# Rebuilt weights made twice as fast, in bursts, and a block's sums taken in three loops, in a linear attention with two feed-forward networks

## The chip, the cores and the metric

The kernel runs on one core of one Trainium2 chip. The metric is the device time of one execution in microseconds (us), as the median of several runs. The engines are named as the profile names them: PE is TensorE (matmul), PEld its weight load, DVE is VectorE, ACT is ScalarE, POOL is GpSimd, and SP is SyncE, whose queue starts nearly all transfers here. Matmuls write to PSUM, which the kernel uses as eight banks of 128 x 512 fp32.

## The reference

A random-feature attention over 4 batches, 8 heads, 576 positions and 64 columns is followed by two feed-forward networks (FFNs) over its 2304 rows of 512.

```
proj = einsum('bhsd,md->bhsm', x, omega);  h = proj - sum(x*x)/2
phi(x) = exp(h - max(h)) / sqrt(128)                  # x = q or k, scaled
kv = einsum('bhsm,bhsd->bhmd', phi(k), v);  z = sum(phi(k), axis=2)
attn = einsum('bhsm,bhmd->bhsd', phi(q), kv) / (phi(q) . z + 1e-6)
x = attn as 2304 x 512
FFN 1: h = x @ w_in (512 x 2048);  g = relu(h)**2;  y = g @ w_out (2048 x 512)
FFN 2: the same with its own weights and g = h if h > 0 else exp(h) - 1
```

The weights of the FFNs come as 64-bit floats, all else as 32-bit floats.

## The kernel before

**Precision.** Each fp32 operand of a large matmul is split into a high and a low limb (`xh`/`xl`, `gh`/`gl`, `wh`/`wl`), and a product is made of three matmuls: high by high, high by low, low by high. The high limb is a copy on ACT, the low limb a subtraction on DVE in the helper `minus` (line 74 in the profile).

**Weights.** The weights are cut into 64 parts (FFN, slice f of 16, and 0 for `w_in` or 1 for `w_out`), each 128 x 512 in 512 KB. `fetch` transfers a part into one of three buffers `st`. A part is then made up in three phases. Phase 0, `make_rebiased`, is one ACT instruction (L122, `cm`). Phase 1, `make_floats`, is three DVE instructions (L129, L130, L133, `cv`), after which the transfer of a later part is issued. Phase 2, `make_limbs`, is the copy to `wh` on ACT (L144) and the subtraction to `wl` on DVE (L74).

**Steps.** The FFNs' work is a list of steps (FFN, group g of 4, block of rows i with its first column n0, slice j of 4). A name such as `gf1_1_0_0_2` carries these five numbers: FFN 1 (the second one), group 1, block 0, column 0, slice 2. In the text a step is written in the same order, and the two networks are "FFN 1" and "FFN 2". A group holds eight parts, and its blocks are four of 512 columns and one of 256 (block 4, which comes second). In the very first group three blocks are taken in halves. `gemm1` of a step makes twelve matmuls into one PSUM bank (`ph`), then an epilogue: r, gf and gh/gl in FFN 1; gf, r, t on ACT, then r and gf on DVE, gh on ACT and gl on DVE in FFN 2. `gemm2` of a step, two steps later, adds twelve matmuls to four PSUM banks (`py`), and after the block's fourth slice the four banks are copied or summed on DVE into pages `ya`. After the last group of FFN 1 the sums become the limbs `xh`/`xl` of FFN 2's input. `moe_pieces` yields after each gemm, so a half step is twelve matmuls.

**Order.** Every engine runs its instructions in the order in which this program text issues them; no scheduler moves them. During attention a list of stages runs once a tick, and from some tick on each tick takes half steps as well. A half step may be followed by phases of weight work: `make(n, phases)` runs a phase if its turn is possible for a part below n. Parts that no gemm uses any more are counted in `n_dead`, and the main loop makes parts up to `n_dead` + 12. `need` makes a missing part on the spot. When a group of eight parts ends, eight new parts may be made.

**Banks.** The eight PSUM banks are handed out in turn to whatever asks next. In the FFNs the four `py` of a block whose `gemm2` starts take, in turn, the banks of three earlier `ph` (free when the epilogue has read them, in FFN 2 with DVE's gf) and of the first `py` of the block before (free when DVE has copied or summed it); the next `ph` takes the second.

Of the kernel before, what the change touches and what calls it, by code (L numbers as in the profile page):

```python
# [12 lines left out]
ALU = mybir.AluOpType  # L13
# [4 lines left out]
def linear_attention_two_ffn_kernel(  # L18
# [12 lines left out]
    nc = tc.nc  # L31
    P = 128
    B, H, S, D = q.shape
# [9 lines left out]
    GF = 4  # L43
    NG = NF // GF
    BLKS = [C * P] * B + [B * L]
# [18 lines left out]
    def page(shape, name, dt=F32):  # L64
        return pages.tile([P] + list(shape), dt, tag="page", name=name)

    def psum(name):
        return ps.tile([P, W], F32, tag="bank", name=name)

    def flat(t):  # L70
        return t.rearrange("p a b -> p (a b)")

    def minus(eng, out, whole, hi):
        eng.tensor_tensor(out=out, in0=whole, in1=hi.bitcast(F32), op=ALU.subtract)  # L74
# [5 lines left out]
    xh, xl = {}, {}  # L80

    def x_pages(moe, i, c, name):

        per = W // BLKS[i]
        for d, s in ((xh, "h"), (xl, "l")):
            if (moe, i, c // per) not in d:
                d[moe, i, c // per] = page([per, BLKS[i]], f"x{s}{moe}_{i}_{c // per}", F32R)
# [7 lines left out]
    parts = [(moe, f, o) for moe in range(2) for f in range(NF) for o in range(2)]  # L95
    parts[:2 * GF] = sorted(parts[:2 * GF], key=lambda p: (p[1] + LOOK * p[2], p[2]))
    staged, w_t = {}, {}
    n_fetched, n_made, n_dead = [0], [0, 0, 0], [0]

    def fetch(n):  # L100
        while n_fetched[0] < min(n, len(parts)):
            moe, f, o = p = parts[n_fetched[0]]
            w = WS[moe][o].bitcast(U32)
            t = stg.tile([P, W, 2], U32, tag="st", name=f"st{moe}_{f}_{o}")
            if o == 0:
                nc.sync.dma_start(
                    out=t.rearrange("p (c f) t -> p c (f t)", c=KD),
                    in_=w[:, f * 2 * P:(f + 1) * 2 * P].rearrange("(c p) f -> p c f", p=P),
                )
            else:  # L110
                nc.sync.dma_start(out=t.rearrange("p f t -> p (f t)"), in_=w[f * P:(f + 1) * P, :])
            staged[p] = t
            n_fetched[0] += 1
# [31 lines left out]
        minus(nc.vector, l, tf, h)  # L145
        w_t[p] = h, l

    def make(n, phases=(2, 1, 0)):

        n = min(n, len(parts))  # L150
        for c in phases:
            if n_made[c] < (n if c == 0 else n_made[c - 1]):
                (make_rebiased, make_floats, make_limbs)[c](n_made[c])
                n_made[c] += 1

    def need(p):
        while p not in w_t:
            make(parts.index(p) + 1)
        return w_t[p]


# [7 lines left out]
    def omega_limbs():  # L169
        nc.vector.tensor_copy(out=om[:, 1, :], in_=om[:, 0, :])  # L170
        p_om = psum("p_om")
        nc.tensor.transpose(p_om[:, :P], flat(om), ident)
        omT = page([2, M], "omT")
        nc.vector.memset(omT, 0.0)
        for j in range(2):
            nc.vector.tensor_scalar(
                out=omT[j * D:(j + 1) * D, j, :], in0=p_om[j * D:(j + 1) * D, :M], scalar1=SCALE, scalar2=None, op0=ALU.mult
            )
        nc.vector.tensor_copy(out=omh, in_=flat(omT))
        minus(nc.vector, oml, flat(omT), omh)  # L180
# [10 lines left out]
    def load(u):  # L191
        b, kind, hp = u
        t = page([8, D], f"ld{b}{kind}{hp}")
        st[u] = {"x": t}
        if kind == "l":
            for n, src in enumerate((k, q)):
                for i in range(LH):
                    nc.sync.dma_start(out=t[i * L:(i + 1) * L, n * NP:(n + 1) * NP, :], in_=left(src, b, i))
        else:
            nc.sync.dma_start(  # L200
                out=t.rearrange("p (h c) d -> p h (c d)", h=2),
                in_=(k if kind == "k" else q)[b, 2 * hp:2 * hp + 2, :C * P, :].rearrange(
                    "h (p c) d -> p h (c d)", c=C
                ),
            )
# [188 lines left out]
    def order(moe, g):  # L394
        whole = [(i, 0, BLKS[i]) for i in range(NB)]
        if (moe, g) == (0, 0):
            return [(i, n, n + W // 2) for i in range(B - 1) for n in (0, W // 2)] + whole[B - 1:]
        if (moe, g) == (1, NG - 1):
            return whole
        return whole[:1] + whole[B:] + whole[1:B]  # L400

    steps = [(moe, g, o, j) for moe in range(2) for g in range(NG) for o in order(moe, g) for j in range(GF)]
    g_t, y_t, ya_t = {}, {}, {}

    def gemm1(moe, g, o, j):
        i, n0, n1 = o
        n = n1 - n0
        nm = f"{moe}_{g}_{i}_{n0}_{j}"
        f = g * GF + j
        ih, il = need((moe, f, 0))  # L410
        ph = psum(f"ph{nm}")
        m = 0
# [29 lines left out]
    def gemm2(moe, g, o, j):  # L442
        i, n0, n1 = o
        n = n1 - n0
        f = g * GF + j
        oh, ol = need((moe, f, 1))
        gh, gl = g_t.pop((moe, g, o, j))
        nt = KD if moe == 0 else n // P
        cols = n if moe == 0 else DM
        per = W // cols  # L450
        if j == 0:
            for t in range(nt // per):
                y_t[t] = psum(f"py{moe}_{g}_{i}_{n0}_{t}")
        for t in range(nt):
            ts = slice(t * P, (t + 1) * P)
            y = y_t[t // per][:, t % per * cols:(t % per + 1) * cols]
            for m, (a, w) in enumerate(((gh, oh), (gh, ol), (gl, oh))):
                nc.tensor.matmul(  # L458
                    y, *((w[:, ts], a) if moe == 0 else (a[:, ts], w)),
                    start=j == 0 and m == 0 and t % per == 0, stop=j == GF - 1 and m == 2, skip_group_check=per > 1,  # L460
                )
        if o == order(moe, g)[-1]:
            n_dead[0] += 1
        if j < GF - 1:
            return
        last = g == NG - 1
        for t in range(nt // per):
            yv = y_t[t]
            if moe == 0 and n < BLKS[i]:
                assert g == 0  # L470
                for u in range(per):
                    c = t * per + u
                    if n0 == 0:
                        ya_t[i, c] = page([W], f"ya{moe}_{i}_{c}")
                    nc.vector.tensor_copy(out=ya_t[i, c][:, n0:n1], in_=yv[:, u * n:(u + 1) * n])
                continue
            if g == 0:
                ya = ya_t[i, t] = page([W], f"ya{moe}_{i}_{t}")
                nc.vector.tensor_copy(out=ya, in_=yv)
                continue  # L480
            ya = ya_t[i, t]
            nc.vector.tensor_tensor(out=ya, in0=yv, in1=ya, op=ALU.add)  # L482
            if not last:
                continue
            ya_t.pop((i, t))
            if moe == 0:
                x_pages(1, i, t * per, "y")
                hi, lo = flat(xh[1, i, t]), flat(xl[1, i, t])
                nc.scalar.copy(out=hi, in_=ya)
                minus(nc.vector, lo, ya, hi)  # L490
            elif i < B:
                nc.sync.dma_start(
                    out=out[i * S:i * S + C * P, :].rearrange("(p c) e -> p c e", c=C)[:, t, :], in_=ya
                )
            else:
                for u in range(P // L):
                    bb = t * (P // L) + u
                    (nc.scalar if u else nc.sync).dma_start(out=out[bb * S + C * P:(bb + 1) * S, :], in_=ya[u * L:(u + 1) * L, :])

    def moe_pieces():  # L500
        for s in range(len(steps) + LOOK):
            if s < len(steps):
                gemm1(*steps[s])
                yield s
            if s >= LOOK:
                gemm2(*steps[s - LOOK])
                yield s
# [7 lines left out]
        (maxima, 3), ("step", 0), (turned, 7), (used, 5), (attended, 6), (load_v, 1),  # L515
    )
    DEPTH = max(d for f, d in stages)
    WEIGHTS, TWO = 2, 25
    work = moe_pieces()
    ready = 0  # L520
    done = -1
    with tc.manual_schedule():
        load(units[0])
        omega_limbs()
        for s in range(1, len(units) + DEPTH):
            for f, d in stages:
                if f == "step":
                    if done + 1 < ready and s >= d * TWO:
                        done = next(work)
                elif f == "weights":  # L530
                    if s >= WEIGHTS:
                        make(2 * GF, ((s - WEIGHTS) % 3,))
                elif 0 <= s - d < len(units):
                    f(units[s - d])
            u = s - DEPTH
            if 0 <= u < len(units) and units[u][1:] == ("q", NP - 1):
                ready += 2 * GF if units[u][0] < B - 1 else GF
        for n, s in enumerate(work):
            make(n_dead[0] + 12, (2 - n % 3,))


# [28 lines left out]
```

## Time and profile before

| | |
|---|---|
| time, median of 3 runs | 1023.67 us (1022.82 to 1023.95) |
| time of the profiled execution | 1023.02 us |
| its span (first to last instruction) | 1021.2 us |
| granted TensorE clock, mean | 0.987 of full |
| PE busy | 980.6 us, 96% of the span |
| DVE busy | 649.9 us, 64% |
| ACT busy | 475.5 us, 47% |
| POOL busy | 71.1 us, 7% |

The profiled execution is one run of the same program with its instructions recorded; the rows further down are from it, in us from the start of its span. Attention fills about the first 135 us, with the first half steps of FFN 1 among it; FFN 1 ends near 607 us. Matmul ends are modelled, so a busy PE is not PE at its peak.

### The profile page before, as it was taken

The page shows a single profiled execution, that of the slowest core. Times are in us where ns is not written, and L with a number is a line of the kernel's source. Part 1 is how long each engine was busy: PE and PEld are TensorE (multiplying, and loading weights), DVE is VectorE, ACT ScalarE, POOL GpSimd, SP SyncE. Part 2 cuts the span into 40 slices and gives each one's busy share as a digit, 9 for nine tenths or more (in the row PEclk, how much of TensorE's full clock was granted, in tenths as well). Part 3 has the DMA queues.
Part 4 walks back from the last instruction along what each step waited for, and adds up shares of the span by engine and source line. Part 5 has one row for each costly group of instructions (what it writes and reads, how often), then busy time and mean ns, then how long its engine had stood idle before and what let it go on. Part 6 is the DMA issues. An engine that isn't in the chain of part 4 may idle for free.

```text
span 1021.2 us, 13964 instructions
## 1 busy us (share of the span) xinstructions
PE 980.6 (96%) x5441; PEld 842.3 (82%) x5441; DVE 649.9 (64%) x1220; ACT 475.5 (47%) x1051; POOL 71.1 (7%) x106
## 2 busy tenths in 40 slices
PE   6999999999989999999999987999999999998998
PEld 5889889999878888888888866888878888886886
DVE  6989766764675546744675566746764786475554
ACT  4777655653433323322343344545554555453443
POOL 5533212200000000000000000000000000000000
PEclk9999989999999999999999998999999999999999
DMA  7442211200222101200220011201210121000111
GB/s 223 130 128 75 75 41 47 73 2 1 62 83 62 42 1 62 83 21 21 63 63 20 1 63 42 62 0 44 81 42 1 63 63 42 1 21 1 52 73 62
DMA packets 56466, 53.37 MB, mean 52 GB/s; under 512 B 25424, under 2 KB 50000, under 8 KB 56400
## 3 DMA queue, kind: packets, MB, share of 16 engines
q1 hardware_dynamic: 56240, 52.21, 16.9%
q8 instruction: 43, 0.70, 0.3%
q10 hardware_dynamic: 160, 0.26, 0.1%
q14 instruction: 23, 0.19, 0.1%
HBM read 47.74 MB, written 4.72 MB: 51 GB/s over the span
## 4 chain that ended last, share of the span: by engine, by line
PE 90%; DVE 6%; ACT 2%; issue 0%; DMA 0%; SPq 0%; POOL 0%; DVEq 0%; ACTq 0%; POOLq 0%
PE ph L416 39%; PE py L458 38%; PE pn L342 3%; DVE cv L130 1%; DVE cv L133 1%; PE pk2k L309 1%; PE pk3k L309 1%; PE pk1k L309 1%; PE pp2q L260 1%; DVE ya L482 1%; PE pp3k L260 1%; PE pp3q L260 1%; PE px L373 1%; PE pk0k L309 1%; DMA st<-in_moe_w_in_dram 0%
## 5 line engine op out<-in xcount | busy, mean ns | idle before, releaser
L416 PE MATMUL ph<-xh,wh 128*128 128x512 f32 (+1 forms) x688 | 248.0, 361 | 16.0 <-ACT wh L144 15.9
L416 PE MATMUL ph<-xh,wl 128*128 128x512 f32 (+1 forms) x688 | 247.4, 360 | 0.1
L416 PE MATMUL ph<-xl,wh 128*128 128x512 f32 (+1 forms) x688 | 247.5, 360 | 0.0
L416 PEld LDWEIGHTS ph<-xh,wh 128*128 128x128 f32 x688 | 130.2, 189 | 39.0 <-ACT wh L144 17.2
L427 ACT ACTIVATE r<-ph 128x512 f32<-128x512 f32 (+1 forms) x92 | 46.6, 507 | 229.1 <-PE ph L416 227.3
L416 PEld LDWEIGHTS ph<-xh,wl 128*128 128x128 f32 x688 | 130.5, 190 | 22.0 <-DVE wl L74 1.2
L416 PEld LDWEIGHTS ph<-xl,wh 128*128 128x128 f32 x688 | 130.4, 190 | 21.0
L74 DVE TENSOR_TENSOR gl<-gf,gh 128x512 fp32r<-128x512 f32 (+1 forms) x172 | 104.2, 606 | 61.5 <-ACT gh L438 51.1
L429 DVE TENSOR_TENSOR gf<-r 128x512 f32<-128x512 f32 (+1 forms) x92 | 52.9, 575 | 138.0 <-ACT r L427 137.7
L458 PE MATMUL py<-gh,wh 128*128 128x512 f32 (+1 forms) x368 | 129.3, 351 | 3.8 <-ACT wh L144 3.8
L458 PE MATMUL py<-gh,wl 128*128 128x512 f32 (+1 forms) x368 | 127.7, 347 | 0.4 <-DVE wl L74 0.2
L458 PE MATMUL py<-gl,wh 128*128 128x512 f32 (+1 forms) x368 | 127.4, 346 | 0.0
L458 PE MATMUL py<-wh,gh 128*128 128x512 f32 x288 | 113.6, 395 | 0.0
L458 PE MATMUL py<-wl,gh 128*128 128x512 f32 x288 | 113.5, 394 | 0.0
L458 PE MATMUL py<-wh,gl 128*128 128x512 f32 x288 | 113.3, 393 | 0.0
L436 DVE SCALAR_TENSOR_TENSOR r<-r,t 128x512 f32<-128x512 f32 (+1 forms) x80 | 51.0, 637 | 95.6 <-ACT t L435 95.6
L438 ACT CAST gh<-gf 128x512 fp32r<-128x512 f32 (+1 forms) x80 | 46.2, 578 | 131.3 <-DVE gf L437 131.3
L458 PEld LDWEIGHTS py<-gh,wh 128*128 128x128 f32 x368 | 69.9, 190 | 13.9 <-ACT wh L144 4.4
L433 ACT ACTIVATE gf<-ph 128x512 f32<-128x512 f32 (+1 forms) x80 | 44.2, 553 | 76.8 <-PE ph L416 76.8
L458 PEld LDWEIGHTS py<-gh,wl 128*128 128x128 f32 x368 | 69.8, 190 | 10.4 <-DVE wl L74 1.0
L458 PEld LDWEIGHTS py<-gl,wh 128*128 128x128 f32 x368 | 69.7, 189 | 9.1
L482 DVE TENSOR_TENSOR ya<-py,ya 128x512 f32<-128x512 f32 x108 | 68.7, 682 | 1.4 <-PE py L458 1.4
(320 smaller groups left out, 1463.0 us busy)
## 6 DMA issues: line engine op xcount, KB each, us to landing
st<-in_moe_w_in_dram SPq DMA_DIRECT2D x32, 512.0 KB, 3.6
st<-in_moe_w_out_dram SPq DMA_DIRECT2D x32, 512.0 KB, 3.5
out_dram<-ya SPq DMA_DIRECT2D x16, 256.0 KB, 2.4
ld0k<-in_k_dram SPq DMA_DIRECT2D x4, 256.0 KB, 5.6
v0k<-in_v_dram SPq DMA_DIRECT2D x8, 128.0 KB, 5.6
ld0q<-in_q_dram SPq DMA_DIRECT2D x4, 256.0 KB, 5.7
ld1k<-in_k_dram SPq DMA_DIRECT2D x4, 256.0 KB, 4.5
v1k<-in_v_dram SPq DMA_DIRECT2D x8, 128.0 KB, 4.6
```

Of the source, the lines that this page charges most:

```text
L74: eng.tensor_tensor(out=out, in0=whole, in1=hi.bitcast(F32), op=ALU.subtract)
L260: nc.tensor.matmul(pp[:, i * 2 * M:(i + 1) * 2 * M], a[:, cs], o, start=(n == 0), stop=(n == 2))
L309: nc.tensor.matmul(o, phs[h][:, c, :], st[u]["v"][:, h * C + c, :], start=False, stop=c == C - 1, skip_group_check=True,)
L342: nc.tensor.matmul(pn[:, c * (D + 1):(c + 1) * (D + 1)], st[u]["qT"][h][:, c, :], st[b, "k", hp]["kv"][:, h, :], start=True, stop=True,)
L416: nc.tensor.matmul(ph[:, :n], wt[:, cs], x_part(xt, moe, i, c)[:, n0:n1], start=(m == 0), stop=(m == 3 * KD - 1))
L427: nc.scalar.activation(out=r, in_=ph[:, :n], func=AF.Relu)
L429: nc.vector.tensor_tensor(out=gf, in0=r, in1=r, op=ALU.mult)
L433: nc.scalar.activation(out=gf, in_=ph[:, :n], func=AF.Relu, scale=-1.0)
L436: nc.vector.scalar_tensor_tensor(out=r, in0=r, scalar=1.0, in1=t, op0=ALU.add, op1=ALU.mult)
L438: nc.scalar.copy(out=gh, in_=gf)
L458: nc.tensor.matmul(y, *((w[:, ts], a) if moe == 0 else (a[:, ts], w)), start=j == 0 and m == 0 and t % per == 0, stop=j == GF - 1 and m == ...
L482: nc.vector.tensor_tensor(out=ya, in0=yv, in1=ya, op=ALU.add)
```

## The change

Three things are changed. First, `make` no longer takes a list of phases but a number of turns: each turn is the next phase in a global rotation 2, 1, 0, and a turn whose phase is not possible is passed over. The main loop takes two turns a half step where it took one phase; `need` takes one turn at a time. Second, in attention the weight work starts at tick 6 (`WEIGHTS`) where it was tick 2; at tick 4 the transfers of two parts are issued without any phase; and each tick takes one or two turns (even, odd) where it was one. Third, at the end of a block the sums, the high limbs and the low limbs are three loops over the block's tiles where they were one.

```diff
-    def make(n, phases=(2, 1, 0)):
+    turn = [0]
+
+    def make(n, phases):
 
         n = min(n, len(parts))
-        for c in phases:
+        for _ in range(phases):
+            c = 2 - turn[0] % 3
+            turn[0] += 1
             if n_made[c] < (n if c == 0 else n_made[c - 1]):
                 (make_rebiased, make_floats, make_limbs)[c](n_made[c])
                 n_made[c] += 1
 
     def need(p):
         while p not in w_t:
-            make(parts.index(p) + 1)
+            make(parts.index(p) + 1, 1)
         return w_t[p]
...
-            ya = ya_t[i, t]
-            nc.vector.tensor_tensor(out=ya, in0=yv, in1=ya, op=ALU.add)
-            if not last:
-                continue
-            ya_t.pop((i, t))
-            if moe == 0:
+            else:
+                nc.vector.tensor_tensor(out=ya_t[i, t], in0=yv, in1=ya_t[i, t], op=ALU.add)
+        if not last:
+            return
+        yas = [ya_t.pop((i, t)) for t in range(nt // per)]
+        if moe == 0:
+            for t, ya in enumerate(yas):
                 x_pages(1, i, t * per, "y")
-                hi, lo = flat(xh[1, i, t]), flat(xl[1, i, t])
-                nc.scalar.copy(out=hi, in_=ya)
-                minus(nc.vector, lo, ya, hi)
-            elif i < B:
+                nc.scalar.copy(out=flat(xh[1, i, t]), in_=ya)
+            for t, ya in enumerate(yas):
+                minus(nc.vector, flat(xl[1, i, t]), ya, flat(xh[1, i, t]))
+            return
+        for t, ya in enumerate(yas):
+            if i < B:
...
-    WEIGHTS, TWO = 2, 25
+    WEIGHTS, TWO = 6, 25
...
                 elif f == "weights":
+                    if s == WEIGHTS - 2:
+                        fetch(2)
                     if s >= WEIGHTS:
-                        make(2 * GF, ((s - WEIGHTS) % 3,))
+                        make(2 * GF, 1 + s % 2)
...
         for n, s in enumerate(work):
-            make(n_dead[0] + 12, (2 - n % 3,))
+            make(n_dead[0] + 12, 2)
```

The order of PE's and POOL's instructions stays as it was; those of DVE, ACT and SP move. In the rows below a name ends in a buffer number of its own.

On ACT, at the start of the program, `th0k0` is the copy of the first transposed heads of k and `cm0_0_0` is phase 0 of the first part. Before:

```order
L122 ACT_TABLE_LOAD
L122 ACTIVATE cm0_0_0_106<-st0_0_0_104 128x512
L246 CAST th0k0_118<-pt0k0_113 128x512
L246 CAST th0l0_148<-pt0l0_143 128x512
L144 CAST wh0_0_0_174<-cv0_0_0_130 128x512
```

After:

```order
L250 CAST th0k0_114<-pt0k0_109 128x512
L250 CAST th0l0_136<-pt0l0_131 128x512
L250 CAST th0q0_176<-pt0q0_171 128x512
...
L328 COPY qT0l0_1_320<-pq0l0_1_321 128x512
L122 ACTIVATE cm0_0_0_331<-st0_0_0_162 128x512
L250 CAST th0k2_343<-pt0k2_338 128x512
```

The first weight's phase 0 has moved from the head of ACT's queue behind thirteen other entries, some of them of four instructions.

On DVE, where the last block of FFN 1 ends, `ya` are the sums and `xl` the low limbs. Before:

```order
L133 SCALAR_TENSOR_TENSOR cv1_3_0_6616<-cm1_3_0_6573,cv1_3_0_6616 128x512
L482 TENSOR_TENSOR ya0_3_0_4006<-py0_3_3_0_0_6487,ya0_3_0_4006 128x512
L74 TENSOR_TENSOR xl1_3_0_6636<-ya0_3_0_4006,xh1_3_0_6635 128x512
L482 TENSOR_TENSOR ya0_3_1_4008<-py0_3_3_0_1_6488,ya0_3_1_4008 128x512
L74 TENSOR_TENSOR xl1_3_1_6641<-ya0_3_1_4008,xh1_3_1_6640 128x512
L482 TENSOR_TENSOR ya0_3_2_4010<-py0_3_3_0_2_6489,ya0_3_2_4010 128x512
L74 TENSOR_TENSOR xl1_3_2_6646<-ya0_3_2_4010,xh1_3_2_6645 128x512
L482 TENSOR_TENSOR ya0_3_3_4012<-py0_3_3_0_3_6490,ya0_3_3_4012 128x512
```

After:

```order
L133 SCALAR_TENSOR_TENSOR cv1_4_1_6652<-cm1_4_1_6621,cv1_4_1_6652 128x512
L485 TENSOR_TENSOR ya0_3_0_4034<-py0_3_3_0_0_6503,ya0_3_0_4034 128x512
L485 TENSOR_TENSOR ya0_3_1_4036<-py0_3_3_0_1_6504,ya0_3_1_4036 128x512
L485 TENSOR_TENSOR ya0_3_2_4038<-py0_3_3_0_2_6505,ya0_3_2_4038 128x512
L485 TENSOR_TENSOR ya0_3_3_4040<-py0_3_3_0_3_6506,ya0_3_3_4040 128x512
L74 TENSOR_TENSOR xl1_3_0_6675<-ya0_3_0_4034,xh1_3_0_6674 128x512
L74 TENSOR_TENSOR xl1_3_1_6678<-ya0_3_1_4036,xh1_3_1_6677 128x512
L74 TENSOR_TENSOR xl1_3_2_6681<-ya0_3_2_4038,xh1_3_2_6680 128x512
```

Four sums now stand together and the low limbs behind them; and the part whose floats come just ahead is (1,4,1) where it was (1,3,0).

On DVE, in FFN 2, between the epilogues of steps (1,1,0,0,0) and (1,1,0,0,1), where the first group has just ended (`cv` and `wl` are weight work). Before:

```order
L436 SCALAR_TENSOR_TENSOR r1_1_0_0_0_7444<-r1_1_0_0_0_7444,t1_1_0_0_0_7445 128x512
L437 TENSOR_TENSOR gf1_1_0_0_0_7441<-r1_1_0_0_0_7444,ph1_1_0_0_0_7428 128x512
L74 TENSOR_TENSOR gl1_1_0_0_0_7443<-gf1_1_0_0_0_7441,gh1_1_0_0_0_7442 128x512
L74 TENSOR_TENSOR wl1_6_1_7454<-cv1_6_1_7408,wh1_6_1_7453 128x512
L129 TENSOR_SCALAR cv1_7_0_7469<-st1_7_0_7334 128x512
L130 SCALAR_TENSOR_TENSOR cv1_7_0_7469<-st1_7_0_7334,cv1_7_0_7469 128x512
L133 SCALAR_TENSOR_TENSOR cv1_7_0_7469<-cm1_7_0_7426,cv1_7_0_7469 128x512
L436 SCALAR_TENSOR_TENSOR r1_1_0_0_1_7491<-r1_1_0_0_1_7491,t1_1_0_0_1_7492 128x512
L437 TENSOR_TENSOR gf1_1_0_0_1_7488<-r1_1_0_0_1_7491,ph1_1_0_0_1_7475 128x512
```

After:

```order
L440 SCALAR_TENSOR_TENSOR r1_1_0_0_0_7472<-r1_1_0_0_0_7472,t1_1_0_0_0_7473 128x512
L441 TENSOR_TENSOR gf1_1_0_0_0_7469<-r1_1_0_0_0_7472,ph1_1_0_0_0_7456 128x512
L74 TENSOR_TENSOR gl1_1_0_0_0_7471<-gf1_1_0_0_0_7469,gh1_1_0_0_0_7470 128x512
L129 TENSOR_SCALAR cv1_8_0_7481<-st1_8_0_7399 128x512
L130 SCALAR_TENSOR_TENSOR cv1_8_0_7481<-st1_8_0_7399,cv1_8_0_7481 128x512
L133 SCALAR_TENSOR_TENSOR cv1_8_0_7481<-cm1_8_0_7450,cv1_8_0_7481 128x512
L74 TENSOR_TENSOR wl1_8_0_7502<-cv1_8_0_7481,wh1_8_0_7501 128x512
L129 TENSOR_SCALAR cv1_8_1_7505<-st1_8_1_7436 128x512
L130 SCALAR_TENSOR_TENSOR cv1_8_1_7505<-st1_8_1_7436,cv1_8_1_7505 128x512
L133 SCALAR_TENSOR_TENSOR cv1_8_1_7505<-cm1_8_1_7487,cv1_8_1_7505 128x512
L440 SCALAR_TENSOR_TENSOR r1_1_0_0_1_7527<-r1_1_0_0_1_7527,t1_1_0_0_1_7528 128x512
L441 TENSOR_TENSOR gf1_1_0_0_1_7524<-r1_1_0_0_1_7527,ph1_1_0_0_1_7511 128x512
```

Between the two epilogues stand the floats of two parts and one low limb, where there stood the floats and the low limb of one part.

## Rows read from the trace of the kernel before

**Rows 1.** Part 1 of the page: busy time of each engine.

```profile
PE 980.6 (96%) x5441; PEld 842.3 (82%) x5441; DVE 649.9 (64%) x1220; ACT 475.5 (47%) x1051; POOL 71.1 (7%) x106
```

**Rows 2.** Windows: stretch; busy of PE, PEld, DVE, ACT, POOL; PEclk; DMA share; GB/s.

```profile
25.00:50.00 25.00, 22.71 (x187) 22.14 (x186) 23.76 (x55) 19.22 (x61) 15.58 (x23) 0.93 0.48 132
130.00:135.00 5.00, 4.68 (x23) 4.39 (x24) 3.44 (x8) 2.67 (x10) 1.23 (x2) 0.58 0.00 0
690.00:720.00 30.00, 30.00 (x131) 24.26 (x131) 21.76 (x35) 16.67 (x29) 0.00 (x0) 1.00 0.15 53
```

**Rows 3.** The waits of PE: line, waited for: total, times, longest.

```profile
PE ph L416 <- ACT wh L144: 15.9, 3, 10.2
PE pp0k L260 <- ACT th0k L246: 4.5, 1, 4.5
PE py L458 <- ACT wh L144: 3.8, 2, 2.3
```

**Rows 4.** Timeline of PE near 708: start, duration, operation, idle before.

```profile
707.00 0.39 PE L458 MATMUL py<-wh,gh 128*128 128x512 f32 x1
...
709.77 0.40 PE L416 MATMUL ph<-xh,wh 128*128 128x512 f32 x1
```

**Rows 5.** Timeline of DVE and PE where FFN 1 ends.

```profile
606.82 0.68 DVE L482 TENSOR_TENSOR ya<-py,ya 128x512 f32<-128x512 f32 x1
...
608.79 0.68 DVE L482 TENSOR_TENSOR ya<-py,ya 128x512 f32<-128x512 f32 x1
...
618.98 0.79 PE L416 MATMUL ph<-xh,wh 128*128 128x512 f32 x1 [10.17 <-ACT wh L144]
...
623.39 0.40 PE L458 MATMUL py<-wh,gh 128*128 128x512 f32 x1
```

**Rows 6.** Timeline of PE at three late weights.

```profile
303.54 0.50 PE L416 MATMUL ph<-xh,wh 128*128 128x512 f32 x1 [2.67 <-ACT wh L144]
...
308.19 0.45 PE L458 MATMUL py<-gh,wh 128*128 128x512 f32 x1
...
318.24 0.50 PE L458 MATMUL py<-gh,wh 128*128 128x512 f32 x1 [1.43 <-ACT wh L144]
...
925.01 0.50 PE L416 MATMUL ph<-xh,wh 128*128 128x512 f32 x1 [3.05 <-ACT wh L144]
...
929.80 0.39 PE L458 MATMUL py<-wh,gh 128*128 128x512 f32 x1
```

**Rows 7.** Timeline of PE and ACT at the start.

```profile
3.96 1.12 PE L243 MATMUL pt0k<-ident,ld0k 128*128 128x128 f32 x4 [0.77 <-DMA ld0k<-in_k_dram]
...
10.42 0.66 ACT L122 ACTIVATE cm<-st 128x512 f32<-128x512 f32 x1 [8.40 <-DMA st<-in_moe_w_in_dram]
```

**Rows 8.** Timeline of PE at the end of attention.

```profile
125.61 0.66 PE L373 MATMUL px<-ident,xs 128*128 128x128 f32 x4 [1.48 <-DVE tl2q L74]
...
130.17 0.58 PE L458 MATMUL py<-gh,wh 128*128 128x256 f32 x1 [2.35 <-ACT wh L144]
```

**Rows 9.** Timeline of DVE, first to second group of FFN 2.

```profile
695.02 2.48 DVE L479 COPY ya<-py 128x512 f32<-128x512 f32 x4
697.41 0.42 DVE L129 TENSOR_SCALAR cv<-st 128x512 uint32<-128x512 uint32 x1
...
699.20 0.68 DVE L436 SCALAR_TENSOR_TENSOR r<-r,t 128x512 f32<-128x512 f32 x1
...
701.29 0.69 DVE L74 TENSOR_TENSOR gl<-gf,gh 128x512 fp32r<-128x512 f32 x1 [0.69 <-ACT gh L438]
...
711.72 0.69 DVE L74 TENSOR_TENSOR wl<-cv,wh 128x512 fp32r<-128x512 f32 x1
712.32 0.42 DVE L129 TENSOR_SCALAR cv<-st 128x512 uint32<-128x512 uint32 x1
...
715.29 0.69 DVE L437 TENSOR_TENSOR gf<-r,ph 128x512 f32<-128x512 f32 x1
```

**Rows 10.** Part 5 of the page: groups by line, busy and mean ns.

```profile
L429 DVE TENSOR_TENSOR gf<-r 128x512 f32<-128x512 f32 (+1 forms) x92 | 52.9, 575 | 138.0 <-ACT r L427 137.7
```

More of the change, by code (lines that the diff above doesn't have):

```diff
@@ L466, in gemm2 @@
         last = g == NG - 1
+        half = moe == 0 and n < BLKS[i]
         for t in range(nt // per):
             yv = y_t[t]
-            if moe == 0 and n < BLKS[i]:
+            if half:
                 assert g == 0
@@ L475, in gemm2 @@
                     nc.vector.tensor_copy(out=ya_t[i, c][:, n0:n1], in_=yv[:, u * n:(u + 1) * n])
-                continue
-            if g == 0:
+            elif g == 0:
                 ya = ya_t[i, t] = page([W], f"ya{moe}_{i}_{t}")
                 nc.vector.tensor_copy(out=ya, in_=yv)
-                continue
-            ya = ya_t[i, t]
-            nc.vector.tensor_tensor(out=ya, in0=yv, in1=ya, op=ALU.add)
-            if not last:
-                continue
-            ya_t.pop((i, t))
-            if moe == 0:
-                x_pages(1, i, t * per, "y")
-                hi, lo = flat(xh[1, i, t]), flat(xl[1, i, t])
-                nc.scalar.copy(out=hi, in_=ya)
-                minus(nc.vector, lo, ya, hi)
-            elif i < B:
+            else:
[5 more added lines that the diff above has]
+            for t, ya in enumerate(yas):
+                x_pages(1, i, t * per, "y")
+                nc.scalar.copy(out=flat(xh[1, i, t]), in_=ya)
[4 more added lines that the diff above has]
+            if i < B:
                 nc.sync.dma_start(
```

## The prediction

> **What bounds the kernel now.** The page's busy line comes first: PE works 980.6 of 1021.2 us, DVE 649.9 [rows 1]. So about 40 us can be had, and an edit to DVE's, ACT's or SP's work is worth only what it does to PE's idle time. The windows show that this share is no average of equals: in 25 to 50 us DVE is busy 23.76 of 25 and PE 22.71, while in 690 to 720 us PE never rests and DVE, though it makes weights there, has 8 us free [rows 2]. The list of PE's waits then names the largest reasons: three waits at gemm 1 for a weight's high limb (15.9 us together, one of 10.2), one of 4.5 for `th0k` at the start, three at gemm 2 for a high limb (3.8) [rows 3]. No wait of PE for a PSUM bank stands among them. A full-speed half step of twelve matmuls takes 2.77 us, from 707.00 to 709.77 [rows 4]; this is my yardstick for what a disturbed half step cost.
>
> **The change part by part.**
>
> *The join of the FFNs.* DVE's sums begin at 606.82, the second at 608.79: a pitch of 1.97, since each low limb stands between two sums and waits for ACT's copy [rows 5]. The epilogue of the next step, and the high limb of weight (1,3,0) behind it, queue behind all four. PE starts gemm 1 of step (1,0,0,0,3) at 618.98 after an idle of 10.17 that begins at 608.81 (by the pitch of the matmuls it could have started at 608.65), and runs that half step until 623.39 instead of 2.77, its first matmul at 0.79 [rows 5]. In all this place costs 623.39 - 608.65 - 2.77 = 12.0 (1.6 of it in the half step itself). After the change the weight is six or more half steps early, so the first wait is gone. The four sums take 2.4 from about 607.45 (a `wl` of 0.61 now stands ahead), so the last PSUM bank is free at 609.85; the four low limbs follow without gaps (2.45). What is late next is `gh` of step (1,0,0,0,3): DVE does 2.4 + 2.45, `wl` 0.61, a wait of 0.6, an epilogue 2.7, weight floats 1.8, `wl` 0.61 with a wait of 0.75, floats 1.8, then r and gf 1.44, and ACT the copy, 0.65: 623.25. PE, with two half-length gemm 1 (256 columns) between, wants it at 620.0. I charge 3.2 for that and 2.1 for bank waits and half clock as below: 5.3. Net **-6.7** (bounds -12 with no new wait, -1 if it is 11).
>
> *Late weights elsewhere.* At 303.54 PE waited 2.67 and then took 308.19 - 303.54 = 4.65 for a half step (1.88 too long); the next weight cost 1.43 at 318.24. At 925.01 it waited 3.05 and took 929.80 - 925.01 = 4.79 (2.02 too long) [rows 6]. In the changed order the last phase of every weight of the FFNs stands at least six half steps ahead of its first use, so all of it goes: **-6.0** and **-5.1**. The slow half steps are the clock: the stretch 130 to 135 us, right behind two waits, has a granted clock of 0.58 [rows 2], between full and the lower level, 1.2 GHz; each of the three idles was followed by 1.6 to 2.0 of loss.
>
> *The start.* ACT's first instruction is the `cm` of the first weight, which sits 8.40 us for the 512 KB transfer and starts at 10.42; `th0k` is queued behind it although PE began its transposes at 3.96 [rows 7]. Now `th0k` is ACT's first, and SP issues `ld0q` ahead of the weights. PE's wait of 4.5 goes, unless the next load is late by as much. But DVE, 95% busy in 25 to 50 us, gets four weights in ticks 7 to 16 where it had about three; some is given back. **-4** (bounds -7, if the loads also come sooner, and +1).
>
> *The end of attention.* PE waits 1.48 at 125.61 for `tl2q`, behind weight work on DVE, and 2.35 at 130.17 for a `wh` [rows 8], and has the 0.58 clock behind. Now two or more phases run per tick and the weight is a tick early. 2.35 and part of the rest: **-4** (bounds -6, 0).
>
> *What is added.* Eight weights a group are now made in some 12 half steps, not 24. A weight is 1.79 of floats (697.41 to the next instruction at 699.20) plus a `wl` of 0.61 (711.72 to 712.32); an FFN 2 epilogue 2.7 (699.20 to the end of gl, 701.29 + 0.61); four copies 2.39 (695.02 to 697.41) [rows 9]. From the first group of FFN 2 to the second, DVE has between 695.02 and gf of step (1,1,0,0,1) six floats (10.7) where there were three, five `wl` (3.05) where there were two, the copies, three epilogues (8.1) and r and gf (1.42): 25.7. `wl` and r also wait on ACT, whose `wh` now sits ahead of the next step's first activation: 0.5 to 1.1 each time, 3.1 in all. gf ends at 723.8, where it ended at 715.98 [rows 9]. gf frees the bank in which gemm 2 of step (1,1,0,0,0) puts its third tile; That gemm 2 starts three half steps after 709.77 [rows 4], at 718.1, and comes to its third tile halfway, at 719.5. So PE waits 4.3, then 2.3 for the copy that frees the fourth (726.9 against 724.5), about 0.8 more at the next block, and 1.0 of half clock: **+8.4**. From the second group to the third the same count gives 1.2 for a gf, 3.1 for the first sum and 1.6 of clock: **+5.9**. From the third to the fourth half the weights remain, and no bank is late. In FFN 1 the epilogue on DVE is two instructions (gf, 575 ns, and gl) [rows 10], and gf needs no bank: ACT's r has freed it. Counted through in the same way from the start of the burst, the sums there are done at 35.1 us and the bank is wanted at 38.2: 0.
>
> The Trainium skill (Perfetto Trace Analysis, Identifying Performance Opportunities) says that gaps which repeat on the engine that should be saturated can mean that SBUF or PSUM ran out for the next tile. It speaks against the burst; the list of waits shows no such gap yet. Without the two bank terms the sum would be some 14 us lower.
>
> Sum: -6.7 - 6.0 - 5.1 - 4 - 4 + 8.4 + 5.9 = -11.5 against 1023.02 of the profiled execution, or 1011.5. The median of the runs is 0.65 above it: **1012**.
>
> **The rivals.** (a) *The bursts do not stall.* The walk is tight: with ACT's copies a little earlier, each stall shrinks, and DVE has 8 of 30 us free in 690 to 720 [rows 2]. Against it: 7.2 us more work before one gf. Then the join gives its 12.0 and nothing is added: -12.0 - 6.0 - 5.1 - 8 = -31, **992**. (b) *DVE and ACT pace PE for the whole burst (slower).* Three FFN 2 steps with four weights are 3 x 2.7 + 4 x 2.4 + 1.8 of copies = 19.5 and up to 2.5 of waits for ACT, 22 against PE's six half steps, 16.6. Two such rounds in a burst are 11, with clock loss up to 16 at each of two transitions: -25.8 + 32 = +6, **1029**. It turns slower once the two cost more than the 25.8 of all gains. For it: waits alternate between the engines and PE idles to half clock; against: eight banks let PE run ahead, and the burst ends. (c) *Attention gives nothing.* DVE is full to 100 us, so weights there only change places with other work: -11.5 + 8 = -3.5, **1020**, or worse by a few us if the two weights a tick push `tl` and the maxima back.
>
> **How the numbers follow.** Chances: forecast 0.57 (own range 1002 to 1018), (a) 0.15, (b) 0.13, (c) 0.15. What this measurement tells from no change is 0.2%, 2.0 us. Faster by more: all of (a), nearly all of the forecast, 0.1 of (c), in all 0.80; within: 0.06; slower: (b) and a little of (c), 0.14. From 995 to 1022 leaves out half of (a) and most of (b).
>
> **What would show it.** In the changed profile: ACT's first instruction reads `pt0k` and starts near 5 us; no wait of PE for `wh` above 1 us after 150 us; four sums of 0.68 in a row on DVE near 593, then four low limbs without gaps; the half step behind 0.50 rather than 0.39 matmuls gone at the two late weights. PE's list of waits should now have gemm 2 waiting for DVE's gf, copies and sums, some 7 us at the first change of group in FFN 2 and 4 at the second, and 3 for `gh` at the join. If PE idles less than 2 us in these, it is (a); if over 10 at each, (b). If PE's windows of 25 to 125 us are not busier than before, (c). The prediction is wrong if a weight still comes late or if the first loads, not `th0k`, hold the start.

## The result, and the profile after

The changed kernel took 1010.58 us (median of 4 runs, 1008.31 to 1011.34) beside 1023.81 for the kernel before: a ratio of 0.986, 95% interval 0.983 to 0.989. The forecast was 1012. The profiled execution took 1011.34 us with a span of 1009.5, 11.7 less than before.

First the page's busy line and PE's list of waits of the changed kernel (line, what it waited for, total, times, longest).

```profile
PE 977.2 (97%) x5441; PEld 838.2 (83%) x5441; DVE 650.4 (64%) x1220; ACT 479.2 (47%) x1051; POOL 70.3 (7%) x106
```

```profile
PE py L462 <- DVE gf L441: 4.8, 2, 4.1
PE py L462 <- ACT gh L442: 2.8, 1, 2.8
PE py L462 <- DVE ya L485: 2.8, 1, 2.8
...
PE py L462 <- DVE ya L483: 1.4, 1, 1.4
```

The waits for a weight's high limb (`wh`) and for `th0k` that led the list in [rows 3] are gone altogether. In their place stand waits of gemm 2 for DVE's gf, sums (`ya L485`) and copies (`ya L483`), which free PSUM banks, and for `gh`: 11.8 us in all.

PE's order is the same in both kernels, so the start of the same half step can be compared in the two traces, and the difference tells what each place gave. The timelines of PE, of the changed kernel, at the half steps that answer to 130.17 [rows 8], 308.19 [rows 6], 623.39 [rows 5] and 929.80 [rows 6]:

```profile
125.47 0.36 PE L462 MATMUL py<-gh,wh 128*128 128x256 f32 x1
...
296.75 0.40 PE L462 MATMUL py<-gh,wh 128*128 128x512 f32 x1
...
598.21 0.39 PE L462 MATMUL py<-wh,gh 128*128 128x512 f32 x1
...
918.24 0.39 PE L462 MATMUL py<-wh,gh 128*128 128x512 f32 x1
```

They stand 4.7, 11.4, 25.2 and 11.6 us sooner: the kernel gains 25 us up to the join and gives 18 of it back in the two group changes of FFN 2 and at the join, before the last late weight brings 5. By place:

| place | foretold, us | measured, us |
|---|---|---|
| start, up to the first half step | -4 | -3.9 |
| rest of attention, weights among full ticks | in the two terms around it | +3.7 |
| end of attention | -4 | -6.6 |
| first to second group of FFN 1 | -6.0 | -6.9 |
| join | -6.7 | -6.7 |
| first to second group of FFN 2 | +8.4 | +8.2 |
| second to third group of FFN 2 | +5.9 | +5.4 |
| third to fourth group of FFN 2 | -5.1 | -4.8 |
| all else | 0 | -0.1 |
| sum | -11.5 | -11.7 |

The timeline at the start, ACT and PE of the changed kernel, answers to [rows 7]: `th0k` is ACT's first operation, as soon as the transposes end, and the projections start at 6.80 instead of 11.61. Then PE waits for the next loads.

```profile
5.07 0.59 ACT L250 CAST th0k<-pt0k 128x512 fp32r<-128x512 f32 x1 [3.06 <-PE pt0k L247]
...
6.80 0.56 PE L264 MATMUL pp0k<-omh,th0k 128*128 128x256 f32 x1
...
13.86 0.63 PE L247 MATMUL pt0k<-ident,ld0k 128*128 128x128 f32 x4 [2.00 <-DMA ld0k<-in_k_dram]
```

Between the first and the eighth half step most of the start's 3.9 is given back. Windows (stretch; busy of PE, PEld, DVE, ACT, POOL; clock; DMA share; GB/s) from the start of the first to the start of the eighth, before:

```profile
73.10:114.80 41.70, 40.66 (x351) 39.81 (x352) 36.17 (x89) 32.56 (x97) 15.30 (x22) 1.00 0.32 91
```

and after, with the two largest of PE's waits there:

```profile
69.20:114.50 45.30, 41.75 (x350) 39.91 (x351) 41.41 (x93) 34.37 (x103) 17.87 (x24) 1.00 0.39 108
```

```profile
PE py L462 <- DVE xl L74: 1.0, 1, 1.0
PE pt1q L247 <- DVE tl1k L74: 0.9, 1, 0.9
```

For the same half steps DVE works 5.2 us more than before. PE's listed waits in this stretch come to 3.7 us, all for DVE, where before they came to 1.0. The prediction's sign for rival (c), windows of PE from 25 to 125 us that are not busier than before, is there:

```profile
25.00:125.00 100.00, 94.69 (x806) 91.61 (x804) 88.94 (x215) 73.85 (x227) 39.56 (x55) 0.98 0.37 104
```

```profile
25.00:125.00 100.00, 91.41 (x780) 87.13 (x780) 93.91 (x217) 72.55 (x218) 38.04 (x54) 1.00 0.40 112
```

The sign was badly chosen, since what attention gains lies ahead of this stretch and behind it. From 125 to 150 us PE never rests:

```profile
125.00:150.00 25.00, 25.00 (x219) 25.00 (x218) 18.16 (x45) 16.58 (x52) 6.21 (x10) 1.00 0.19 49
```

The new stalls, from the timelines of DVE and PE. The four sums take one row of 2.48 and the low limbs one of 2.49 where [rows 5] had a pitch of 1.97 for one tile; `gh` is then late by 2.81, the third bank by 4.13, the fourth by 1.41, and one group later a bank by 0.64 and one by 2.81.

```profile
593.87 2.48 DVE L485 TENSOR_TENSOR ya<-py,ya 128x512 f32<-128x512 f32 x4
596.27 2.49 DVE L74 TENSOR_TENSOR xl<-ya,xh 128x512 fp32r<-128x512 f32 x4
...
609.58 0.51 PE L462 MATMUL py<-wh,gh 128*128 128x512 f32 x1 [2.81 <-ACT gh L442]
...
702.86 0.69 DVE L441 TENSOR_TENSOR gf<-r,ph 128x512 f32<-128x512 f32 x1
...
703.60 0.79 PE L462 MATMUL py<-wh,gh 128*128 128x512 f32 x1 [4.13 <-DVE gf L441]
...
706.66 0.79 PE L462 MATMUL py<-wh,gh 128*128 128x512 f32 x1 [1.41 <-DVE ya L483]
...
808.61 0.50 PE L462 MATMUL py<-wh,gh 128*128 128x512 f32 x1 [0.64 <-DVE gf L441]
...
812.38 0.79 PE L462 MATMUL py<-wh,gh 128*128 128x512 f32 x1 [2.81 <-DVE ya L485]
```

The waits are not all of a stall. The two at the first change of group in FFN 2 are 5.5 of its 8.2; the rest lies in slow matmuls, in a stretch with a granted clock of 0.52, close to the lower of its two levels (1.2 and 2.4 GHz):

```profile
703.00:710.00 7.00, 4.98 (x11) 3.50 (x12) 5.86 (x10) 3.90 (x7) 0.00 (x0) 0.52 0.22 71
```

### The profile page after: what moved, and what is told of

Same layout as the page of the kernel before. It is cut to its first block, busy times and chain, and to the rows that moved or that the text cites. A ratio compares the mean times of both kernels' runs of the same rounds, so it can differ in the third digit from the quotient of the medians.

```text
span 1009.5 us, 13991 instructions
## 1 busy us (share of the span) xinstructions
PE 977.2 (97%) x5441; PEld 838.2 (83%) x5441; DVE 650.4 (64%) x1220; ACT 479.2 (47%) x1051; POOL 70.3 (7%) x106
## 4 chain that ended last, share of the span: by engine, by line
PE 79%; DVE 14%; ACT 3%; issue 1%; DMA 1%; SPq 1%; POOL 0%; DVEq 0%; POOLq 0%; ACTq 0%
PE ph L420 35%; PE py L462 35%; PE pn L346 2%; DVE cv L130 1%; DVE wl L74 1%; DVE cv L133 1%; DVE gf L441 1%; DVE r L440 1%; ACT gh L442 1%; DVE cv L129 1%; PE pk3k L313 1%; PE pk2k L313 1%; ACT wh L144 1%; DMA ld0q<-in_q_dram 1%; DVE gl L74 1%
## 5 line engine op out<-in xcount | busy, mean ns | idle before, releaser
L462 PE MATMUL py<-wh,gh 128*128 128x512 f32 x288 | 115.8, 402 | 12.0 <-DVE gf L441 4.8
L462 PEld LDWEIGHTS py<-wh,gh 128*128 128x128 f32 x288 | 54.7, 190 | 27.0 <-DVE gf L441 5.6
```

Source lines behind the costliest of these rows:

```text
L462: nc.tensor.matmul(y, *((w[:, ts], a) if moe == 0 else (a[:, ts], w)), start=j == 0 and m == 0 and t % per == 0, stop=j == GF - 1 and m == ...
```

## The experiments

The theory under test: the weights' rate removes late weights, attention gives some 7 us, the loops serve the join alone, and the burst's new stalls are DVE's backlog. Rivals: one part carries all, or the stalls come from the banks' order, whatever DVE does. Ratios are to the kernel before, with 95% intervals.

**The three loops alone** (`e1_sums`): the kernel before with the last part of the diff only.

> The kernel before with the three loops alone (weights at one phase a half step, attention as before). My theory: a term only at the join of the FFNs, where the four sums and four low limbs take 2.4 + 2.45 us on DVE instead of 7.9, so the epilogue and the high limb behind them come 3.0 us sooner and PE's wait of 10.17 for that weight shrinks to about 7; all else stays, late weights too: 1020.7 us. The rival that the loops alone carry the gain at the join expects the wait to be gone there, -10 to -12, about 1012. The rival that the order of the sums is hidden expects 1023.7.

Measured: 1019.71 us, ratio 0.995 (0.994 to 0.997). The join gave 3.9, where 3.0 were worked out, and no other place behind attention moved; attention, which is the same program, took 1.2 longer in this execution. The late weight still held PE for 6.0 of the 10.17:

```profile
PE ph L416 <- ACT wh L144: 11.8, 3, 6.0
```

So the loops shorten the join's queue and do not carry the gain.

**Two phases per half step alone** (`e2_two`): the kernel before with

```diff
-            make(n_dead[0] + 12, (2 - n % 3,))
+            make(n_dead[0] + 12, (2 - 2 * n % 3, 2 - (2 * n + 1) % 3))
```

> The kernel before with two phases per half step in the main loop alone (attention and the sums as before). My theory: the late weights go (-6.9 at the first change of group in FFN 1, -4.8 at the last in FFN 2, both as in the changed kernel), the two new stalls of FFN 2 come (+8.2 and +5.4), and the join loses its 12.0 but waits longer for gh, banks and clock than in the changed kernel, about 9 instead of 5, as the sums still alternate with the low limbs: net -3. Sum -1, about 1022.5 us. The rival that the rate alone explains the gain expects the join as in the changed kernel, -4.9 in all, about 1018.8 or lower.

Measured: 1027.89 us, ratio 1.003 (1.001 to 1.005): slower. The late weights went (-6.7 and -3.3) and the new stalls came (+5.5 and +5.6), but the join cost 2.9 more than in the kernel before, not 3 less: gemm 2 there waited 4.08 for a gf before the sums had even begun, which my working had not in it, then 2.10 for a sum and 2.82 for `gh`.

```profile
605.29 0.50 PE L458 MATMUL py<-wh,gh 128*128 128x512 f32 x1 [4.08 <-DVE gf L437]
```

Doubling the rate is therefore worth nothing by itself.

**The changed attention alone** (`e3_attn`): the changed kernel with the sums as before and

```diff
-            make(n_dead[0] + 12, 2)
+            make(n_dead[0] + 12, 1)
```

> The changed kernel with one turn per half step in the main loop and the sums as before, so that only attention is changed. My theory: the first half step starts 3.9 us sooner, most of that is given back up to the last third of attention, where weights now stand in ticks in which DVE is full, and 6.5 come back at the end of attention, where no weight is late: -6.8 in all; the three late weights behind attention stay. 1016.9 us. The rival that attention gives nothing in the end (DVE full) expects 1022 to 1024.

Measured: 1004.97 us, ratio 0.981 (0.977 to 0.984), faster than the whole change. Attention gave 8.6, but the waits for a weight at the join and at the last group were gone as well, and one had come at the second group of FFN 2. This broke part of the theory: the rate is not what those two waits needed. Nor is all that the join gives back the doubled rate's: at one turn per half step, with the sums as before, it gave back 5.1 here, and as much in the shifted rotation below, behind a wait for `gh`:

```profile
607.13 0.50 PE L462 MATMUL py<-wh,gh 128*128 128x512 f32 x1 [1.65 <-ACT gh L442]
```

**1.5 turns per half step** (`e4_1p5`): the changed kernel with `make(n_dead[0] + 12, 1 + n % 2)`.

> The changed kernel with one and two turns in alternation per half step in the main loop, 1.5 on average (after: 2). My theory: the stalls in FFN 2 are DVE's backlog in the burst. Three steps then hold three weights, 8.1 + 7.2 + 1.8 = 17.1 us of DVE and some waits against PE's 16.6, not 19.5: the stalls of 8.2 and 5.4 fall to about 2 and 1, that at the join from 4.9 to about 3, and no weight comes late again. About 1010.6 - 12 = 998.5 us. The rival that the stalls come from how the banks are handed out, whatever the rate, expects 1010 again; the rival that 1.5 is too slow expects waits for a high limb at the changes of group, and 1008 or more.

Measured: 996.8 us, ratio 0.973 (0.970 to 0.976). No wait for a weight; the stalls of 8.2 and 5.4 shrank to 2.4 each, in waits of 1.2 or less, and the join gave 9.6 instead of 6.7:

```profile
695.66 0.50 PE L462 MATMUL py<-wh,gh 128*128 128x512 f32 x1 [1.10 <-DVE ya L483]
```

The mean granted clock of the profiled execution is 1.00, where it was 0.992 with two turns, so little is lost to slow matmuls. Of the 15 us between the two profiles 2.6 lie in attention, which is the same program. The rival that the banks' order makes the stalls, whatever the rate, falls: the banks are handed out the same.

**Low limbs of weights on POOL** (`e5_pool`): the changed kernel with

```diff
-        minus(nc.vector, l, tf, h)
+        minus(nc.vector if n < 2 * GF else nc.gpsimd, l, tf, h)
```

> The changed kernel with the subtraction for a weight's low limb on POOL instead of DVE, outside attention; POOL is otherwise idle there. My theory: PE's new stalls are DVE's backlog in the bursts. Without five subtractions (3.05 us) and their waits for ACT (some 1.5) ahead of gf, the first stall of FFN 2 (8.2) and the second (5.4) fall to under 1 each and the join gives some 2: 1010.6 - 14 = 996.5 us. The rival that the banks' order or ACT makes the stalls expects 1010 again. The rival that POOL slows DVE at the shared memory (the floats took 1.10 to 1.42 us instead of 0.69 beside POOL in attention) expects about half of it, 1003.

Measured: 1008.71 us, ratio 0.984 (0.982 to 0.987): 2 us, not 14. gf was late by 3.73 instead of 4.13. The groups of DVE's weight work in the stretch that ends with this gf (busy, mean ns) show where the gain went, first in the changed kernel from 674.8 to 703.5, then with POOL from 674.3 to 702.6:

```profile
L133 DVE SCALAR_TENSOR_TENSOR cv<-cm,cv 128x512 uint32<-128x512 uint32 x6 | 4.1, 691 | 0.2
L74 DVE TENSOR_TENSOR wl<-cv,wh 128x512 fp32r<-128x512 f32 x5 | 3.4, 688 | 1.8 <-ACT wh L144 1.8
L129 DVE TENSOR_SCALAR cv<-st 128x512 uint32<-128x512 uint32 x6 | 2.5, 419 | 0.0
```

```profile
L133 DVE SCALAR_TENSOR_TENSOR cv<-cm,cv 128x512 uint32<-128x512 uint32 x6 | 5.9, 991 | 0.4
...
L129 DVE TENSOR_SCALAR cv<-st 128x512 uint32<-128x512 uint32 x6 | 3.6, 606 | 0.0
```

Five low limbs of 3.4 us are gone from DVE, and the floats take 2.9 more beside POOL. The timeline (DVE and ACT, the burst) shows a second thing, a chain between the engines:

```profile
690.86 0.69 DVE L133 SCALAR_TENSOR_TENSOR cv<-cm,cv 128x512 uint32<-128x512 uint32 x1
...
693.92 0.69 DVE L440 SCALAR_TENSOR_TENSOR r<-r,t 128x512 f32<-128x512 f32 x1 [2.37 <-ACT t L439]
```

```profile
691.59 0.62 ACT L144 CAST wh<-cv 128x512 fp32r<-128x512 f32 x1 [2.58 <-DVE cv L133]
...
693.28 0.61 ACT L439 ACTIVATE t<-gf 128x512 f32<-128x512 f32 x1
```

ACT's `wh` waits for floats that DVE has only just made; gf, r and t of the next step queue behind it; DVE's r waits for t. Without the low limbs' waits for `wh` (1.8) DVE waits longer at this r (2.37 for 1.0), so the chain costs it nearly as much as before.

**The rotation shifted** (`e6_shift`): the kernel before with `(2 - (n + 2) % 3,)` for `(2 - n % 3,)`.

> The kernel before with the main loop's rotation of phases shifted by two half steps and nothing else. New theory after the run with attention alone, which lost the waits at the join and at the last group though its rate is one turn per half step: where a late weight costs anything is an accident of where the rotation stands when a group ends, since a weight's last phase then falls one, two or three half steps ahead of its use, and only one (in FFN 2) costs 5 us or more. Shifted, the first weight of the join and that of the last group have three, that of the second group of FFN 2 has one: join -7, last group -5.2, first group of FFN 1 -3.2, second group of FFN 2 +5.1: -10, about 1013.5 us. The rival that the earlier weights of attention took these waits away expects 1023.7 here.

Measured: 1012.47 us, ratio 0.988 (0.985 to 0.991). One number in the kernel before is worth nearly as much as the whole change. The waits of 10.17 and 3.05 [rows 5, 6] are gone, the late weights of FFN 1's second group gave 6.3, and one wait came where a weight now is late, 4.8 with its slow half step:

```profile
712.22 0.80 PE L416 MATMUL ph<-xh,wh 128*128 128x512 f32 x1 [3.03 <-ACT wh L144]
```

**Without the three loops** (`e7_nosums`): the changed kernel with the sums as before.

> The changed kernel with the sums, high limbs and low limbs of a tile together again, as before. My theory: at the join gh of step (1,0,0,0,3) comes 7.9 - 4.85 = 3.0 us later and banks up to 3.5 later, nothing else moves: the join's new loss of 4.9 grows to 8 to 9, so 1014 us. The rival that this part is hidden by the two phases expects 1010.6. The rival that the bank waits add to it as in the kernel before with two phases, where the join cost 15, expects 1020.

Measured: 1016.77 us, ratio 0.993 (0.990 to 0.995), 6.2 more than the changed kernel. In the profiles the join costs 5.2 more and the next stall 1.0. The half steps there show the bank waits that the loops spare: gemm 2 2.59 and gemm 1 0.82 for a sum. The loops matter more at the higher rate than at the lower (3.9 in the first run).

**Both, 1.5 turns and POOL** (`e8_1p5_pool`).

> The changed kernel at 1.5 turns per half step with the weights' low limbs on POOL outside attention: both cures of the backlog at once. My theory: of the stalls that 1.5 turns left in FFN 2 and at the join (waits of 0.5 to 1.2 and half clock, some 8 us in all) about 6 go: 991 us. The rival that POOL costs DVE as much as it takes from it expects 996.8 or more.

Measured: 991.65 us, ratio 0.968 (0.965 to 0.971), the fastest. After 140 us a single wait of PE above 0.3 is left:

```profile
610.99 0.39 PE L420 MATMUL ph<-xh,wh 128*128 128x256 f32 x1 [0.97 <-DVE gf L441]
```

**A part's lag between floats and limbs** (`e9_lag`): the changed kernel, two turns, with

```diff
-            if n_made[c] < (n if c == 0 else n_made[c - 1]):
+            late = len(w_t) >= 2 * GF and c == 2 and n_made[1] < n
+            if n_made[c] < (n if c == 0 else n_made[c - 1] - late):
```

> The changed kernel, same rate and same work, but a part's limbs are made only when the next part's floats have been issued, so that ACT's copy never waits for floats issued just ahead of it. New theory after the run with POOL, which took 3 us of work from DVE and moved the stall of 4.1 by 0.4 only: in the burst DVE's floats, ACT's wh behind them, ACT's three activations behind wh and DVE's r behind those form one chain, and DVE idles for ACT in it (2.4 us at one r in that run). Without the chain DVE runs through: gf of step (1,1,0,0,1) ends some 2.9 us sooner, the first stall of FFN 2 falls from 8.2 to 3 or 4, the second from 5.4 to 2 or 3, the join by 1 to 2: about 1001.5 us. The rival that DVE's amount of work alone makes the stalls expects 1009 to 1011.

Measured: 1000.76 us, ratio 0.977 (0.974 to 0.979). With the same work on DVE in all, and one low limb (0.69) fewer ahead of the first late gf, the first stall fell from 8.2 to 5.0, the second from 5.4 to 1.1, and the join gave 9.1 instead of 6.7; gf was late by 1.01, and the low limb and the r behind it follow the floats without a gap:

```profile
687.17 0.69 DVE L133 SCALAR_TENSOR_TENSOR cv<-cm,cv 128x512 uint32<-128x512 uint32 x1
687.78 0.68 DVE L74 TENSOR_TENSOR wl<-cv,wh 128x512 fp32r<-128x512 f32 x1
688.38 0.68 DVE L441 SCALAR_TENSOR_TENSOR r<-r,t 128x512 f32<-128x512 f32 x1
```

DVE's waits for ACT's `wh` and t in the stretch that ends with the late gf, in the changed kernel (674.8 to 703.5) and with the lag (671.1 to 696.7), fall from 2.8 to 0.4:

```profile
DVE wl L74 <- ACT wh L144: 1.8, 3, 0.7
DVE r L440 <- ACT t L439: 1.0, 1, 1.0
```

```profile
DVE wl L74 <- ACT wh L144: 0.4, 1, 0.4
```

**Lag and POOL** (`e10_lag_pool`).

> The same with the low limbs on POOL outside attention, still two turns per half step. If the chain between the engines hid the gain of POOL before, it shows now: with DVE's work the only limit left, five subtractions less (3.0 us, less what POOL slows DVE, some 1.8) take what is left of the first stall: 996 us, 5 to 6 below the run with the lag alone. The rival that POOL's gain was lost to the shared memory, not to the chain, expects no difference to the run with the lag alone.

Measured: 1005.1 us, ratio 0.982 (0.979 to 0.984): 4.3 slower than the lag alone. My theory falls here and the rival is right, beyond what it said. The groups of DVE's floats from 600 to 1000 us (busy, mean ns), first with the lag alone, then with POOL:

```profile
L133 DVE SCALAR_TENSOR_TENSOR cv<-cm,cv 128x512 uint32<-128x512 uint32 x22 | 15.2, 692 | 1.0
L130 DVE SCALAR_TENSOR_TENSOR cv<-st,cv 128x512 uint32<-128x512 uint32 x22 | 15.2, 692 | 0.8
```

```profile
L133 DVE SCALAR_TENSOR_TENSOR cv<-cm,cv 128x512 uint32<-128x512 uint32 x22 | 24.8, 1127 | 1.7
L130 DVE SCALAR_TENSOR_TENSOR cv<-st,cv 128x512 uint32<-128x512 uint32 x22 | 18.1, 825 | 0.7
```

These two instructions of 22 parts take 12.5 us more on DVE; 22 subtractions, at 0.61 from one start to the next, would have taken 13.4. What POOL takes off DVE here it costs DVE again, nearly all of it. The Trainium skill (SBUF — State Buffer, Who interferes with whom) says that a DVE instruction with two SBUF inputs contends with a GpSimd instruction that reads SBUF. Both these lines have two such inputs, and the rows agree: 1.67 instead of 0.69 where one meets POOL's subtraction.

```profile
685.39 3.27 POOL L74 TENSOR_TENSOR wl<-cv,wh 128x512 fp32r<-128x512 f32 x2 [3.18 <-ACT wh L144]
```

```profile
685.84 1.67 DVE L130 SCALAR_TENSOR_TENSOR cv<-st,cv 128x512 uint32<-128x512 uint32 x1
```

**POOL in attention too** (`e11_pool_all`).

> The changed kernel at 1.5 turns with the low limbs on POOL in attention too (so far outside it only; that run took 991.65 us). In attention the changed kernel gives back 3.7 us of the start's 3.9 between its first half step and the last third. If that is DVE being full there, eight subtractions less (4.9 us) give 2 to 4 of it back: 988 to 990 us. The rival that POOL, busy with its own squares in attention, delays these or slows DVE's floats expects 991.5 or more.

Measured: 995.8 us, ratio 0.972 (0.970 to 0.974), 4.2 slower than without; all of it before the first half step (4.5), and PE now waits 1.6 for POOL's squares. So this does not show that DVE's fullness is what gives the start's gain back; moving its work to POOL makes POOL late. DVE's floats were not slower there (the L133 and L130 of attention took 0.69 on average).

**1.5 turns and the lag** (`e12_1p5_lag`).

> The changed kernel at 1.5 turns per half step with the lag of a part between floats and limbs, all subtractions on DVE. My theory: at 1.5 turns the stalls are short (waits of 0.5 to 1.2, some 8 us in all with the clock), and part of them is the chain between the engines, the rest DVE's amount of work: about half goes, 993 us, between the run at 1.5 turns (996.8) and that with POOL (991.65). The rival that at this rate floats and limbs are mostly apart anyway expects 996.8 again.

Measured: 995.6 us, ratio 0.972 (0.967 to 0.976), 1.2 below 1.5 turns alone, with ranges that overlap; its profile gains 1.0 in each of the two group changes and loses 1.7 in attention, which is the same program. That is two fifths of the 4.8 left in the group changes. Why POOL gave 5 us at 1.5 turns and cost 4 at two with the lag is only partly shown. At 1.5 turns DVE's round per step, gl to gl, was 5.58 with the low limb (which waits 0.39 for ACT there) and 5.48 with POOL, and PE's two half steps are 5.54 [rows 4]: DVE just fails to keep up, then just does. DVE's timeline, at 1.5 turns and with POOL:

```profile
676.50 0.69 DVE L74 TENSOR_TENSOR gl<-gf,gh 128x512 fp32r<-128x512 f32 x1 [0.69 <-ACT gh L442]
...
682.08 0.69 DVE L74 TENSOR_TENSOR gl<-gf,gh 128x512 fp32r<-128x512 f32 x1 [0.69 <-ACT gh L442]
```

```profile
675.15 0.69 DVE L74 TENSOR_TENSOR gl<-gf,gh 128x512 fp32r<-128x512 f32 x1 [0.69 <-ACT gh L442]
...
680.63 0.69 DVE L74 TENSOR_TENSOR gl<-gf,gh 128x512 fp32r<-128x512 f32 x1 [0.69 <-ACT gh L442]
```

## Why the prediction was right

**The two FFN 2 stalls** were foretold at 8.4 and 5.9 and measured at 8.2 and 5.4, by the mechanism given: gf of step (1,1,0,0,1) ended at 703.55, which is 723.8 on the clock of before (20.2 of gain ahead of it), as worked out. The waits were 4.13 (4.3 foretold), 1.41 (2.3), 0.64 (1.2) and 2.81 (3.1). The rule of the Trainium skill (Perfetto Trace Analysis, Identifying Performance Opportunities) on repeated gaps and a full PSUM holds in so far as the gaps are waits for banks; the run at 1.5 turns shows that with the same banks they shrink when DVE, which frees them, has less ahead. More banks were not tried. That the sums came so near is in part luck, since two errors cancel: at the first change of group the waits came to 5.5 for 7.4 foretold (the 0.8 at the next block did not come), and the slow matmuls took 2.7 for 1.0. What the working called DVE's backlog has two parts. One is the chain from DVE's floats through ACT back to DVE: with the lag, which nearly removes it, two fifths of the first stall and four fifths of the second went (8.2 to 5.0, 5.4 to 1.1), a little of it by the low limb put off. I had counted that chain as "0.5 to 1.1 each time, 3.1 in all", and 2.8 were measured. The other part is DVE's work, as the run at 1.5 turns shows.

**The late weights** were priced from their waits and slow half steps and gave 6.9, 4.8 and, at the join, 11.6, of which 4.9 went again (5.3 foretold) with `gh` late by 2.81 (3.2). The sentence that all this needs the weights early is right; that it needs the higher rate, which the prediction took over from the change, is not. The shifted rotation shows it: what cost 10.17 and 3.05 was where the rotation stood when a group ended.

**Attention** was foretold at -8 and gave -6.8; the split was off. The start gave the 3.9 expected, but 3.7 were lost again by the eighth half step, and the end of attention gave 6.6, not 4: the wait of 2.35, the slow half steps behind it, and time that PE had just lost to DVE. Nine kernels with this attention gave 6.8 to 9.4 by its end (that with POOL in attention apart), so a difference of 1 or 2 us between them means little. In these nine the last stretch gave 6.6 each time; what varies is the start (3.4 to 5.6 gained) and what is lost behind it (1.9 to 3.9).

**The rivals.** (a) No stall: refuted by 11.8 us of waits. (b) DVE and ACT pace PE for the whole burst: the chain is there, but 8.2 and 5.4 are about half and a third of the 16 it priced. (c) Attention gives nothing: refuted by the third run, whose difference at the end of attention is 8.6.

**What stays open:** how to keep the start's gain. Between the first and the eighth half step all of PE's listed waits are for DVE, which does 5.2 us more there than before; that this is the weights moved into these ticks was not tested, since the one attempt to relieve DVE made POOL the trouble. Whether the loops at one turn per half step would keep the 5.1 that the join gave back there was not run either.

## What to carry to other kernels

A weight that comes late once per group may be a matter of where a rotation stands, so shift it before raising its rate. When background work is made faster, look for who frees the buffers that the main engine takes next: here the change as a whole paid for 30 us of gain with 18, and 1.5 turns instead of two kept 14 us more. If a stage on one engine feeds a copy on another that feeds the first again, leave a whole part between them: the lag saved 9.8 us at two turns. Before work is moved to another engine, see what the two do to each other's instructions: POOL's subtractions took 3.4 us off DVE in one stretch and put 2.9 back.

## What was not expected of the hardware

POOL's subtraction of 128 x 512 took from 1.26 to 1.86 us, and DVE's floats of 0.69 took up to 1.85 in the runs with it. After a wait PE's next matmul of 512 columns showed 0.50 or 0.79 instead of 0.39, and the length of the wait does not tell which: 0.79 after 4.13 and after the 2.81 for a sum, 0.51 after the 2.81 for `gh`, 0.50 after 4.08 in the run with two phases alone. The one behind 4.13 lies in the stretch with a granted clock of 0.52.
